# Constant matmuls placed before TensorE's pieces in the first pairs of a linear-attention and MLP kernel

## The chip, the cores and the metric

The kernel runs on one core of a Trainium2 chip. The metric is the device time of one execution in microseconds (us). A core has five engines that work beside one another, each through its own instructions in order: TensorE (PE, matrix products; its weight loads are listed as PEld), VectorE (DVE), ScalarE (ACT), GpSimd (POOL) and SyncE (SP), which here only issues DMAs. Engines wait for one another through semaphores.

## The reference

Inputs q, k, v and f_logit have the shape batch 4, heads 8, sequence 768, head dimension 48. For each batch and head a 48 x 48 state is carried along the sequence:

```python
f = 1.0 / (1.0 + np.exp(-f_logit))
for t in range(S):
    state = f[:, :, t, :, None] * state + np.einsum('bhd,bhe->bhde', k[:, :, t], v[:, :, t])
    y[:, :, t] = np.einsum('bhd,bhde->bhe', q[:, :, t], state)
```

The result is laid out as 3072 tokens of 384 numbers (x) and goes through an MLP with w_in (384 x 2048) and w_out (2048 x 384):

```python
h = x @ w_in
g = 0.5 * (h + np.sqrt(h * h + 4.0))
out = g @ w_out
```

## The kernel before

The 3072 tokens are cut into 24 blocks of 128 tokens, r = 0 to 23, and 12 pairs of blocks, p = 0 to 11. The recurrence is computed by blocks. For each pair:

- SP loads f_logit, q, k and v (`add_load`, L376). In the first three pairs each block has its own pieces (`FINE`).
- ACT makes the logarithms of the gates (exp, then ln: L422, L427), and POOL or DVE splits them into two 16-bit parts, lhi and llo (L430, L433).
- PE forms centred sums of these along the block by a product with a constant triangle, wcent (`m1`, L464 and L465), and the small sums of L470 and L471. ACT takes exponentials of both signs, ea and eap (L478). POOL or DVE multiplies q and k by them (L484) and casts v (L491).

Then follows, for each block, the attention (`add_attention`, `add_state`): transposes of q and k into qkT (L587, `tp`; its copy out of PSUM is L591), scores (L612, `sc`), the mask on DVE (L619, pm), the output y (L633 and L635, `yf`), its cast by ACT or DVE (L642, L644), transposes of y (L677, `yt`) copied by L680, and the state's update (L697 and L700, `kv`, and L704 on DVE, sn). Some pairs' transposes are made by DMA instead (`XBAR`, none of the first five pairs). The MLP takes a pair as 256 tokens: the up-projection in eight halves of four engines' pieces (`half`, L734, six matmuls for each of the eight w_in tiles), the square on ACT (L740, hsq), the root on ACT (L749, r), the sum on DVE (L757, g), and the down-projection in quarters (`quarter`, L777), the copy out (L786, L788) and the store (L792). Exponentials and roots need different ACT tables, which are reloaded between stretches (L831, L833).

POOL also issues the DMAs of the weights, eight tiles of w_in and eight of w_out (L400). They stand in POOL's one order between its other pieces; the first of w_in waits for the v cast of pair 1.

The order of all engines is written out by a planner before anything is emitted (`Plan`, L97 to L274). Every piece of work is an `Op` with an engine, an assumed duration, dependencies, buffers that it takes and uses, and a due time. `Plan.run` walks through time with these assumed durations and picks, engine by engine, the piece that can start first, by due time among those that could start almost at once. The result is the list `P.order`; after that the pieces are emitted in this order:

```python
    P.run()
    for op in P.order:
        ...
            op.emit()
```

Each engine then executes its instructions in this fixed order, and the assumed times play no further part. PSUM has eight banks: five in the ring `hps`, used by the centred sums, the up-projection and the first four blocks' attention (`EARLY`), two in `a` for the later attention, one in `o`.

ident16, a 128 x 128 identity of 16 bits, is made by POOL at the very start and is the constant operand of the transposes.

Of the kernel before, what the change touches and what calls it, by code (L numbers as in the profile page):

```python
# [65 lines left out]

LATE = 11

VDMA = False


class Op:
    __slots__ = ("eng", "dur", "deps", "emit", "due", "allocs", "uses", "end", "kind", "dma", "ins", "done", "kin")

    def __init__(self, eng, dur, emit, deps=(), due=0.0, allocs=(), uses=(), kind=None, dma=None, ins=()):
        self.eng, self.dur, self.emit, self.due, self.kind, self.dma = eng, dur, emit, due, kind, dma
# [20 lines left out]
class Plan:  # L97
# [14 lines left out]
    def __init__(self):  # L112
        self.queues = {}
        self.order = []

    def add(self, queue, eng, dur, emit, p=None, at=None, due=0.0, **kw):
        if isinstance(dur, dict):
            eng = FULL[ENG[queue][p if at is None else at]]
            dur = dur[eng]
        due += SHIFT.get(queue, 0.0) + (0.0 if p is None else BASE[PART[queue]][p])  # L120
        op = Op(eng, dur, emit, due=due, **kw)
        op.kin = queue
        self.queues.setdefault((eng, queue), []).append(op)
        return op

    def ready(self, op):
        t = 0.0
        for d in op.deps:
            if d.end is None:
                return None  # L130
            t = max(t, d.end + (0.0 if d.eng == op.eng and d.dma is None else self.HOP))
        for b in op.allocs:
            r = b.ring
            k = len(r.bufs) - r.n
            if r.ordered and b.seq != len(r.bufs):
                return None

            k += sum(1 for x in op.allocs[:op.allocs.index(b)] if x.ring is r)
            if k >= 0:
                for u in r.bufs[k].users:  # L140
                    if u.end is None:
                        return None
                    t = max(t, u.end + (0.0 if u.eng == op.eng and u.dma is None else self.HOP))
        return t

    def transfer(self, streams, t, until):

# [24 lines left out]
    def run(self):  # L172
# [10 lines left out]
        while left:  # L183
            best = None
            for eng, ks in by_eng.items():
                now = free.get(eng, 0.0)
                cands = []
                for k in ks:
                    if heads[k] < len(self.queues[k]):
                        op = self.queues[k][heads[k]]  # L190
# [59 lines left out]
            if eng == "ACT" and op.kind is not None:  # L250
# [5 lines left out]
                if op.kind[0] == "W":  # L256
                    stretch = op.kind[1]
                    if not any(o.kind == op.kind for o in self.queues[k][heads[k] + 1:]):
                        stretch = None
            free[eng] = op.end = t + dur  # L260
            if eng == "DVE" and op.kin in self.PORT:
                locked = op.end
            if op.dma is not None:
# [14 lines left out]
def kernel(  # L278
# [10 lines left out]
    nc = tc.nc  # L289
# [155 lines left out]
    def add_decays(p, g):  # L445
# [11 lines left out]
        for x, y in pieces(p):  # L457
            n = y - x

            def m1(x=x, y=y):  # L460
                for r in range(x, y):
                    T["ca", p, r] = pp_h.tile([128, 512], FP32, name="hps", tag="hps")
                    ca = T["ca", p, r][:, 0:H * D]
                    nc.tensor.matmul(out=ca, lhsT=wcent, rhs=lhi[p % NL][:, r, :, 0:D], start=True, stop=False)  # L464
                    nc.tensor.matmul(out=ca, lhsT=wcent, rhs=llo[p % NL][:, r, :, 0:D], start=False, stop=True)  # L465
                for r in range(x, y):
                    nl = T["ca", p, r][:, H * D:H * D + 2 * NP].rearrange("p (j s) -> p j s", s=2)
                    for hp in range(NP):
                        o = nl[:, hp, :]
                        nc.tensor.matmul(out=o, lhsT=lhi[p % NL][:, r, 2 * hp:2 * hp + 2, :], rhs=hvec, start=True, stop=False)  # L470
                        nc.tensor.matmul(out=o, lhsT=llo[p % NL][:, r, 2 * hp:2 * hp + 2, :], rhs=hvec, start=False, stop=True)  # L471
# [86 lines left out]
    def add_attention(r):  # L558
# [13 lines left out]
        for xbar in (p in XBAR,):  # L572
            if xbar:
                def tx():
                    nc.sync.dma_start_transpose(out=new("qkT", [128, 2 * NP, C], FP16, 3),
                                                in_=qk[p % NB][:, i].rearrange("p a h d -> p (a h d)"))
                t_ops.append(P.add("xq", "SP", 1.2, tx, deps=[g1, g2], p=p, due=due, allocs=[qkT_b], uses=[qk_b, kk_b], dma=(0.9, 1024)))
            else:
                a_b = bank(r)

                def tp():
                    new("qkT", [128, 2 * NP, C], FP16, 3)
                    tr = psum(r, [128, 2 * NP, C], FP16, "tr")
                    T["tr", r] = tr
                    for s in range(2):
                        for j in range(NP):
                            nc.tensor.transpose(out=tr[:, s * NP + j, :], in_=qk[p % NB][:, i, s, 2 * j:2 * j + 2, :],  # L587
                                                identity=ident16)

                def tc_():  # L590
                    cp[tc_ops[r].eng](out=T["qkT", r], in_=T["tr", r])  # L591

                o = P.add("T", "PE", 0.45, tp, deps=[g1, g2], p=p, due=due, allocs=[a_b, qkT_b], uses=[qk_b, kk_b])
                tc_ops[r] = P.add("T", None, {"DVE": 0.69, "ACT": 1.0}, tc_, at=r, deps=[o], p=p, due=due, uses=[a_b])
                t_ops.append(tc_ops[r])
# [8 lines left out]
        def sc():  # L604
            new("pm", [128, 2, NP, C], FP16, 2)
            for s in range(2):
                T["sc", r, s] = psum(r, [128, NP, C], FP32, "sc")
            qkT = T["qkT", r]
            for j in range(NP):
                for s in range(2):  # L610
                    o = 64 * s
                    nc.tensor.matmul(out=T["sc", r, s][:, j, :], lhsT=qkT[o:o + D, NP + j, :], rhs=qkT[o:o + D, j, :],  # L612
                                     start=True, stop=True)
# [13 lines left out]
        def yf():  # L627
            new("y16", [128, NJ, 128], FP16, 3)
            y = psum(r, [128, NP, 2, D], FP32, "y")
            T["y", r] = y  # L630
            for j in range(NP):
                if c > 0:
                    nc.tensor.matmul(out=y[:, j], lhsT=T["qkT", r][:, j, :], rhs=T["sn", r][:, j], start=True, stop=False)  # L633
                for s in range(2):
                    nc.tensor.matmul(out=y[:, j, s], lhsT=T["pm", r][:, s, j, :], rhs=T["v16", p][:, i, 2 * j + s, :],  # L635
                                     start=(c == 0), stop=(c == 0 or s == 1))
# [26 lines left out]
        for xbar in (p in XBAR,):  # L663
            if xbar:
                def yx():
                    xn()
                    nc.sync.dma_start_transpose(out=xo(), in_=T["y16", r].rearrange("p a b -> p (a b)"))
                op = P.add("xy", "SP", 1.2, yx, deps=[yc_op], p=p, due=due + 6.0, allocs=allocs, uses=[y16_b], dma=(0.4, 384))
            else:
                a_b = bank(r)  # L670

                def yt():
                    xn()
                    t = psum(r, [128, NJ, C], FP16, "yt")
                    T["yt", r] = t
                    for j in range(NJ):
                        nc.tensor.transpose(out=t[:, j, :], in_=T["y16", r][:, j, :], identity=ident16)  # L677

                def ytc():
                    nc.vector.tensor_copy(out=xo(), in_=T["yt", r])  # L680

                o = P.add("YT", "PE", 0.17, yt, deps=[yc_op], p=p, due=due + 6.0, allocs=[a_b] + allocs, uses=[y16_b])
                op = P.add("YT", "DVE", 0.35, ytc, deps=[o], p=p, due=due + 6.0, uses=[a_b])
            xT_ops.setdefault(p, []).append(op)

    def add_state(r, p, due):
# [5 lines left out]
        def kv():  # L692
            T["sn", r + 1] = sp.tile([128, NP, 2, D], FP16, name="sn", tag="sn", bufs=2)
            u = psum(r, [128, NP, 2, D], FP32, "u")
            T["u", r] = u
            if c > 0:
                nc.tensor.matmul(out=u.rearrange("p a b d -> p (a b d)"), lhsT=ident16,  # L697
                                 rhs=T["sn", r].rearrange("p a b d -> p (a b d)"), start=True, stop=False)
# [17 lines left out]
    def add_mlp1(p):  # L716
# [3 lines left out]
        for j4 in range(4):  # L720
            hsq_b, r_b = Buf(ring("hsq", 2)), Buf(ring("r16", 2))
            sq, h_bs = [], [Buf(ring("h", NH)) for _ in range(2)]
            for a in range(2):
                j2 = 2 * j4 + a

                def half(j2=j2, first=a == 0):
                    if first:
                        for x in (j2, j2 + 1):
                            T["h", p, x] = pp_h.tile([128, 512], FP32, name="hps", tag="hps")
                    hb = T["h", p, j2].rearrange("p (a t) -> p a t", a=2)  # L730
                    for a in range(2):
                        jn = 2 * j2 + a
# [31 lines left out]
    def add_mlp2(p):  # L764
        for i in range(PR):
# [3 lines left out]
            for n in range(4):  # L769
                def quarter(n=n, i=i):  # L770
                    if n == 0:
                        if p >= LATE:
                            T["o", p, i] = pp_h.tile([128, DM], FP32, name="o", tag="hps")
                        else:
                            T["o", p, i] = pp_o.tile([128, DM], FP32, name="o", tag="o")
                    for jn in range(4 * n, 4 * n + 4):
                        nc.tensor.matmul(out=T["o", p, i], lhsT=T["g", p][:, jn, i * C:(i + 1) * C],  # L777
                                         rhs=w_out16[jn // 2][:, jn % 2, :], start=(jn == 0), stop=(jn == NN - 1))
# [45 lines left out]
    for op in direct_ops:  # L824
        if AFTER[op.kin[1:]] is not None:
            op.deps.append(dec[AFTER[op.kin[1:]], PR - 1][1])

    P.run()
    for op in P.order:
        if op == "exp":  # L830
            nc.scalar.preload_act_table_set("natural_log_exp_and_others")  # L831
        elif op == "sqrt":
            nc.scalar.preload_act_table_set("sqrt_and_others")  # L833
        else:
            op.emit()


# [28 lines left out]
```

## Time and profile before

| | |
|---|---|
| median of 4 runs | 206.98 us (206.68 to 207.39) |
| the profiled execution | 206.59 us, of which the span from first to last instruction is 204.6 us |
| busy PE / ACT / DVE / POOL | 181.8 / 169.1 / 142.5 / 90.9 us |
| granted TensorE clock | 1.000 |
| DMA | 32.09 MB, mean 157 GB/s |

The profile is one execution. Its page gives the busy time of every engine, the span in 40 slices with the busy share in tenths, the chain of waits that ended last, and the costliest groups of instructions. A line such as "22.69 1.03 PE L587 MATMUL tr<-ident,qk ... x8 [3.45 <-POOL qk L484]" in a timeline means: from 22.69 us on, for 1.03 us, PE ran eight matmuls of line 587 that write tr; it had been idle for 3.45 us before, and what ended the wait was POOL's instruction of line 484. The ends of matmuls are modelled and overlap what follows, so the time that a group of matmuls holds PE is read from its start and the start of the next group. A line of the chain gives start, duration and what was at work: an engine with the tile and the line, a DMA, an engine's queue (SPq, POOLq), or "issue", where nothing that the profile shows was waited for. The granted clock in the profile is one number for a window; it need not show all that makes a matmul slow.

### The profile page before, as it was taken

The numbers are of one execution on the slowest core, as the hardware profiler recorded it, in microseconds if no ns is written. First come the engines' busy times: TensorE is split into PE (matmuls) and PEld (weight loads), VectorE is DVE, ScalarE is ACT, GpSimd is POOL, SyncE is SP. The second block draws the span as 40 slices with busy tenths as digits, with TensorE's granted clock in tenths as the row PEclk, the third lists the DMA queues.
The fourth block names the chain that finished last, engine by engine and source line by source line (L and its number), as shares of the span: only waits on it lengthen the run. The fifth ranks groups of instructions, "written<-read, shape, count | busy, mean of one in ns | idle before, by whom it ended". The sixth has DMA issues, their size and how long they took to land.

```text
span 204.6 us, 4831 instructions
## 1 busy us (share of the span) xinstructions
PE 181.8 (89%) x1870; PEld 133.1 (65%) x1870; DVE 142.5 (70%) x286; ACT 169.1 (83%) x271; POOL 90.9 (44%) x103
## 2 busy tenths in 40 slices
PE   0666488889898998999999999999999999999993
PEld 0344366667676576777777777677777877767761
DVE  5656275697765768998498983989828888944720
ACT  4457217989999999999999999999898899967930
POOL 7171599991049396409960059900089100010010
PEclk9999999999999999999999999999999999999999
DMA  6999999999999999999999897999987812121112
GB/s 125 190 187 188 175 185 183 200 218 196 161 202 188 192 221 185 200 159 230 158 196 227 157 203 156 199 199 190 173 136 162 134 27 62 25 93 41 38 38 77
DMA packets 128102, 32.09 MB, mean 157 GB/s; under 512 B 121088, under 2 KB 127360, under 8 KB 128080
## 3 DMA queue, kind: packets, MB, share of 16 engines
q1 hardware_dynamic: 121744, 25.70, 73.7%
q0 software_dynamic: 6336, 6.10, 15.2%
q8 instruction: 14, 0.23, 0.5%
q14 instruction: 8, 0.07, 0.1%
HBM read 25.17 MB, written 4.72 MB: 146 GB/s over the span
## 4 chain that ended last, share of the span: by engine, by line
PE 63%; POOL 8%; ACT 8%; SPq 7%; DMA 6%; issue 4%; DVE 3%; ACTq 0%; POOLq 0%; DVEq 0%
PE o L777 28%; PE hps L734 23%; SPq L376 7%; DMA w_out<-in_moe_w_out_dram 3%; DMA ld_q<-in_q_dram 3%; PE sc L612 3%; POOL w_in L400 2%; POOL qk L484 2%; ACT r L749 2%; ACT hsq L740 2%; PE y L635 2%; POOL llo L433 2%; PE y L633 1%; PE hps L464 1%; PE hps L465 1%
## 5 line engine op out<-in xcount | busy, mean ns | idle before, releaser
L757 DVE SCALAR_TENSOR_TENSOR g<-hps,r 128x512 f16<-128x512 f32 x96 | 62.2, 685 | 17.1 <-ACT r L749 16.4
L777 PE MATMUL o<-w_out,g 128*128 128x384 f16 x384 | 72.3, 326 | 1.2 <-DVE o_sb L788 0.8
L734 PE MATMUL hps<-xT,w_in 128*128 128x256 f16 x576 | 72.7, 277 | 0.7 <-DMA w_in<-in_moe_w_in_dram 0.7
L734 PEld LDWEIGHTS <-w_in 128*128 128x128 f16 x576 | 55.7, 99 | 11.5 <-DMA w_in<-in_moe_w_in_dram 1.0
L740 ACT ACTIVATE hsq<-hps 128x512 f16<-128x512 f32 x96 | 54.1, 593 | 5.6 <-PE hps L734 4.3
L749 ACT ACTIVATE r<-hsq 128x1024 f16<-128x1024 f16 x48 | 50.8, 1059 | 1.4
L777 PEld LDWEIGHTS <-g 128*128 128x128 f16 x384 | 35.3, 97 | 20.4 <-issue 1.6
L619 DVE TENSOR_TENSOR pm<-sc,mask 128x512 f16<-128x512 f32 x48 | 31.3, 684 | 8.4 <-PE sc L612 8.3
L792 POOL DMA_DIRECT2D out_dram<-o_sb x15 | 8.6, 573 | 59.0 <-DVE o_sb L788 43.2
L484 POOL TENSOR_TENSOR qk<-ld_q,ea 128x768 f16<-128x768 f32 (+1 forms) x10 | 15.8, 1584 | 27.0 <-PE hps L471 14.2
L484 POOL TENSOR_TENSOR qk<-ld_k,eap 128x768 f16<-128x768 f32 (+1 forms) x12 | 18.6, 1546 | 0.9 <-ACT eap L478 0.9
L433 POOL TENSOR_TENSOR llo<-ls,lhi 128x768 f16<-128x768 f32 (+1 forms) x12 | 16.8, 1401 | 2.0 <-PE hps L734 1.5
L491 POOL CAST v<-ld_v 128x768 f16<-128x768 f32 (+1 forms) x13 | 8.7, 677 | 17.2 <-DMA ld_v<-in_v_dram 17.2
L704 DVE TENSOR_TENSOR sn<-u,gam 128x384 f16<-128x384 f32 x20 | 11.0, 551 | 7.3 <-PE u L700 6.6
L422 ACT ACTIVATE ld_f<-ld_f 128x768 f32<-128x768 f32 (+1 forms) x15 | 10.9, 724 | 5.4 <-DMA ld_f<-in_f_logit_dram 5.3
L464 PE MATMUL hps<-lhi,wcent 128*128 128x384 f16 x24 | 8.9, 369 | 6.3 <-POOL lhi L430 5.5
L478 ACT ACTIVATE ea<-hps 128x384 f32<-128x384 f32 x24 | 10.9, 500 | 3.2 <-PE hps L471 3.0
L635 PE MATMUL y<-v,pm 128*128 128x48 f16 x192 | 12.3, 190 | 0.9 <-DVE pm L619 0.9
L587 PE MATMUL tr<-ident,qk 128*128 128x128 f16 x80 | 8.2, 265 | 5.3 <-POOL qk L484 4.4
L635 PEld LDWEIGHTS <-pm 128*128 128x128 f16 x192 | 10.6, 102 | 2.9 <-DVE pm L619 1.1
L612 PE MATMUL sc<-qkT 48*128 48x128 f16 x192 | 10.6, 233 | 1.6 <-DVE qkT L591 0.8
L427 ACT ACTIVATE ls<-ld_f 128x768 f32<-128x768 f32 (+1 forms) x15 | 10.8, 717 | 1.0
(55 smaller groups left out, 209.1 us busy)
## 6 DMA issues: line engine op xcount, KB each, us to landing
ld_f<-in_f_logit_dram SPq DMA_DIRECT2D x24, 192.0 KB, 4.7
ld_k<-in_k_dram SPq DMA_DIRECT2D x24, 192.0 KB, 4.6
ld_q<-in_q_dram SPq DMA_DIRECT2D x24, 192.0 KB, 4.3
ld_v<-in_v_dram SPq DMA_DIRECT2D x24, 192.0 KB, 4.4
out_dram<-o_sb POOLq DMA_DIRECT2D x15, 192.0 KB, 3.8
out_dram<-o_sb SPq DMA_DIRECT2D x9, 192.0 KB, 2.0
w_in<-in_moe_w_in_dram POOLq DMA_DIRECT2D x8, 192.0 KB, 6.7
w_out<-in_moe_w_out_dram POOLq DMA_DIRECT2D x8, 192.0 KB, 7.4
```

The source lines that it names most:

```text
L376: (nc.gpsimd if cast else nc.sync).dma_start(out=T["v16" if cast else name, p][:, r], in_=src_of[name][b][:, c * C:(c + 1) * C, :].rearran ...
L433: eng_of[lg[p, x].eng].tensor_tensor(out=llo[p % NL][:, x:y, :, 0:D], in0=T["ls", p][:, x:y], in1=lhi[p % NL][:, x:y, :, 0:D], op=ALU.subt ...
L484: eng_of[mu[p, x, i].eng].tensor_tensor(out=qk[p % NB][:, x:y, i, :, 0:D], in0=T[name, p][:, x:y], in1=T[e, p][:, x:y], op=ALU.mult)
L612: nc.tensor.matmul(out=T["sc", r, s][:, j, :], lhsT=qkT[o:o + D, NP + j, :], rhs=qkT[o:o + D, j, :], start=True, stop=True)
L619: nc.vector.tensor_tensor(out=T["pm", r][:, s], in0=T["sc", r, s], in1=mask16.unsqueeze(1).broadcast_to([128, NP, C]), op=ALU.mult)
L635: nc.tensor.matmul(out=y[:, j, s], lhsT=T["pm", r][:, s, j, :], rhs=T["v16", p][:, i, 2 * j + s, :], start=(c == 0), stop=(c == 0 or s == 1))
L704: nc.vector.tensor_tensor(out=T["sn", r + 1], in0=T["u", r], in1=gam[b % 2][:, c].unsqueeze(3).broadcast_to([128, NP, 2, D]), op=ALU.mult)
L734: nc.tensor.matmul(out=hb[:, a, :], lhsT=w_in16[j2][:, j, a * 128:(a + 1) * 128], rhs=T["xT", p][:, j, :], start=(j == 0), stop=(j == NJ - 1))
L740: nc.scalar.activation(out=T["hsq", p, j4][:, a], in_=T["h", p, j2], func=AF.Square, scale=1.0)
L749: nc.scalar.activation(out=T["r16", p, j4], in_=T["hsq", p, j4], func=AF.Sqrt, scale=0.25, bias=1.0)
L757: nc.vector.scalar_tensor_tensor(out=T["g", p][:, jn:jn + 2, :].rearrange("p a t -> p (a t)"), in0=T["h", p, 2 * j4 + a], scalar=0.5, in1= ...
L777: nc.tensor.matmul(out=T["o", p, i], lhsT=T["g", p][:, jn, i * C:(i + 1) * C], rhs=w_out16[jn // 2][:, jn % 2, :], start=(jn == 0), stop=( ...
```

## The change

The planner stores the planned start of each piece. A new method, `warm`, then walks through PE's pieces in their order and gives each a number, `heat`, by the idle time that the plan shows ahead of it: the first piece gets 0.8 of its gap at 0.08 us each, later ones 0.7 of a gap over 0.3 us at 0.058 us each, as long as they start before 45 us in the plan. When a PE piece is emitted, as many products of the identity with itself are put before it, into the PSUM tile that the piece is about to write. The real matmul starts its accumulation anew, so the products leave nothing behind. Before the transposes (`tp`, `yt`) they are transposes of the identity, elsewhere 128 x 128 matmuls of 128 columns. The orders of all engines stay as they were.

```diff
+WARM = 45.0
...
+    def warm(self):
+
+
+        end = 1.6
+        for op in self.order:
+            if not isinstance(op, str) and op.eng == "PE":
+                gap = op.start - end
+                if end < 2.0:
+                    op.heat = int(0.8 * gap / 0.08)
+                elif gap > 0.3 and op.start < WARM:
+                    op.heat = int(0.7 * gap / 0.058)
+                end = op.start + op.dur
...
             free[eng] = op.end = t + dur
+            op.start = t
...
                     ca = T["ca", p, r][:, 0:H * D]
+                    if r == x:
+                        heat(ca[:, 0:C])
                     nc.tensor.matmul(out=ca, lhsT=wcent, rhs=lhi[p % NL][:, r, :, 0:D], start=True, stop=False)
...
                     T["tr", r] = tr
+                    for _ in range(P.heat):
+                        nc.tensor.transpose(out=tr[:, 0, :], in_=ident16, identity=ident16)
...
                 T["sc", r, s] = psum(r, [128, NP, C], FP32, "sc")
+            heat(T["sc", r, 0][:, 0, :])
...
             T["y", r] = y
+            heat(y.rearrange("p a b d -> p (a b d)")[:, 0:C])
...
                     T["yt", r] = t
+                    for _ in range(P.heat):
+                        nc.tensor.transpose(out=t[:, 0, :], in_=ident16, identity=ident16)
...
             T["u", r] = u
+            heat(u.rearrange("p a b d -> p (a b d)")[:, 0:C])
...
                             T["h", p, x] = pp_h.tile([128, 512], FP32, name="hps", tag="hps")
+                    heat(T["h", p, j2][:, 0:C])
...
+                        heat(T["o", p, i][:, 0:C])
...
+    def heat(t):
+        for _ in range(P.heat):
+            nc.tensor.matmul(out=t, lhsT=ident16, rhs=ident16, start=True, stop=True)
+
     P.run()
+    P.warm()
...
+            P.heat = op.heat
             op.emit()
```

In the emitted program this makes 246 products, 492 rows with their weight loads, before 20 of PE's pieces. In PE's order they stand as follows:

| before | products |
|---|---|
| centred sums of block 0, block 1 | 49, 8 |
| transposes, scores of block 0 | 14 (transposes), 13 |
| transposes of block 1, y of block 0 | 6 (transposes), 9 |
| y, transposes of y of block 1 | 10, 12 (transposes) |
| transposes, scores of block 2 | 17 (transposes), 13 |
| state's update by block 2, y of block 2 | 5, 5 |
| y, transposes of y of block 3 | 17, 11 (transposes) |
| centred sums of block 5 | 12 |
| up-projection of pair 0: second, third tile | 6, 6 |
| y of block 4 | 13 |
| up-projection of pair 0: fifth tile | 17 |
| up-projection of pair 1: first tile | 3 |

More of the change, by code (lines that the diff above doesn't have):

```diff
@@ L67 @@
 LATE = 11
+WARM = 45.0
 VDMA = False
 class Op:
-    __slots__ = ("eng", "dur", "deps", "emit", "due", "allocs", "uses", "end", "kind", "dma", "ins", "done", "kin")
+    __slots__ = ("eng", "dur", "deps", "emit", "due", "allocs", "uses", "end", "kind", "dma", "ins", "done", "kin", "heat", "start")
     def __init__(self, eng, dur, emit, deps=(), due=0.0, allocs=(), uses=(), kind=None, dma=None, ins=()):
@@ L114, in __init__ @@
         self.order = []
+        self.heat = 0
     def add(self, queue, eng, dur, emit, p=None, at=None, due=0.0, **kw):
@@ L122, in add @@
         op.kin = queue
+        op.heat = 0
         self.queues.setdefault((eng, queue), []).append(op)
```

## The prediction

> **What bounds the kernel now.** I read the page first (shares and the 40 slices), then the chain of waits in order of time for the first 70 us, then the timelines of TensorE (PE), ScalarE (ACT) and GpSimd (POOL) there, and last what SyncE's (SP) queue waits for.
>
> ```profile
> PE 181.8 (89%) x1870; PEld 133.1 (65%) x1870; DVE 142.5 (70%) x286; ACT 169.1 (83%) x271; POOL 90.9 (44%) x103
> ...
> PE   0666488889898998999999999999999999999993
> ```
>
> A slice is 5.1 us. PE is idle at the start and nearly full from the tenth slice on: the change works only where PE has room, in the first 45 us. Who sets the time there is told by the chain:
>
> ```profile
> 15.96 5.55 DMA ld_q<-in_q_dram
> ...
> 21.64 0.79 POOL qk L484
> ...
> 37.64 0.71 POOL w_in L400
> 38.38 1.66 POOL llo L433
> 40.03 0.67 POOL w_out L400
> 40.70 6.88 DMA w_out<-in_moe_w_out_dram
> ...
> 47.62 0.48 PE o L777 x2
> 48.10 1.32 PE hps L734 x12
> 49.45 0.61 ACT hsq L740
> 50.08 1.06 ACT r L749
> ```
>
> The chain has no PE in its first 47 us. It runs through SP's loads to a landing at 21.5, through POOL's work and weight issues to 40.7, through a weight's landing to 47.6, then through ACT to 69 and PE to the end. PE in that time:
>
> ```profile
> 22.69 1.03 PE L587 MATMUL tr<-ident,qk 128*128 128x128 f16 x8 [3.45 <-POOL qk L484]
> 23.52 0.53 PE L697 MATMUL u<-sn,ident 128*128 128x384 f16 x1
> ...
> 33.03 2.72 PE L734 MATMUL hps<-xT,w_in 128*128 128x256 f16 x12
> 35.54 1.06 PE L587 MATMUL tr<-ident,qk 128*128 128x128 f16 x8
> ...
> 42.35 0.61 PE L587 MATMUL tr<-ident,qk 128*128 128x128 f16 x8
> 42.80 0.82 PE L734 MATMUL hps<-xT,w_in 128*128 128x256 f16 x6
> 44.30 0.83 PE L734 MATMUL hps<-xT,w_in 128*128 128x256 f16 x6 [0.69 <-DMA w_in<-in_moe_w_in_dram]
> ```
>
> Take starts, not durations. Eight transposes take 0.83 us at 22.69 (104 ns each) but 0.45 at 42.35 (56 ns); twelve up-projection matmuls take 2.51 us at 33.03 (209 ns each) but 1.31 later (109 ns). So PE runs at about half speed until some 37 us and at full speed after, though the granted clock reads 1.000 in every window. And in the last row PE waits for a weight.
>
> ```profile
> 31.30 0.48 ACT L642 CAST y<-y 128x384 f16<-128x384 f32 x1 [3.85 <-PE y L635]
> ...
> 33.21 0.49 ACT L478 ACTIVATE ea<-hps 128x384 f32<-128x384 f32 x1 [0.65 <-PE hps L471]
> ...
> 45.17 0.60 ACT L740 ACTIVATE hsq<-hps 128x512 f16<-128x512 f32 x1 [0.49 <-PE hps L734]
> ```
>
> These are ACT's only waits between 31 and 57 us; it is dense otherwise (22.8 of 24 us busy from 33 to 57). The last one is the weight of 44.30 passed on.
>
> **The change part by part.** It removes and reorders nothing. On PE it puts 246 constant products (186 matmuls, 60 transposes) ahead of 20 of the planned pieces. By the transposes' rows one costs 56 ns on a fast PE and 104 ns on a slow one: 13.8 or 25.6 us in all. DMAs, queues and the other engines' instructions are the same. What is queued behind a product is the real piece that it stands before, so lateness is what counts.
>
> *To 22.7 us: 138 products (49, 8, 14, 13, 6, 9, 10, 12, 17).* The first need only the identity, ready at 1.30. PE's idle pieces before 22.69 are 5.55 + 0.91 + 0.79 + 0.93 + 0.51 + 0.65 + 3.45 = 12.8 us, 11.5 after 1.30. Fast, 138 x 56 ns = 7.7 us fit. All slow, 14.4 us leave 2.9 us of lateness at the transposes of 22.69. I take no lateness: 49 products in a row are 5.1 us even when slow, longer than the 4 us of dense work from 33.03 after which PE was seen fast. What hides any small lateness is the landing of ld_q at 21.5, for which POOL sat idle 5.33 us; SP's queue ahead of it waits only for earlier DMAs. Nothing can be gained before that landing either.
>
> *22.7 to 33 us: 63 products (13, 5, 5, 17, 11, 12).* Fast they cost 3.5 us. PE is busy 8.34 of these 10.3 us at half speed; at full speed some 4 us go, and waits of 0.46 + 0.93 + 0.57 us take products too. So the y piece before ACT's 31.30 comes perhaps 1 us earlier. What is late next is POOL: the centring matmul of the next block needs llo, which POOL ends at 32.34, and it already started at 32.45. So ACT's ea at 33.21 gains about 0.3 us. POOL itself waits for none of this: its qk at 33.09 starts when its weight issue ends, 0.5 us after ACT's eap is done. All slow, 63 x 104 = 6.6 us less the 2.0 us of waits make the 33.21 row 4.6 us later.
>
> *33 to 45 us: 42 products (6, 6, 13, 17) and 3 more.* At 56 ns the 42 cost 2.35 us. Speed gives back 12 x 100 ns at 33.03, 8 x 48 ns at 35.54, and of the 1.42 us of the next six matmuls all but 6 x 109 ns: 1.2 + 0.4 + 0.8 = 2.4 us. They cancel, and a wait of 0.75 us at 40.08 holds the 13. PE reaches the last up-projection weight no later than before and stands there until it lands. Its issue is POOL's at 37.57, behind POOL work without a gap from 25.5 us on. So the 0.49 us wait of ACT stays or grows by the 0.3 us gained above, and 45.17 is unmoved. The 3 last products (0.17 us) precede matmuls that end at 46.0 for a square at 46.76: hidden; without that cover 0.17 us.
>
> *From 45 us on* PE's instructions are the same. The second down-projection weight still lands at 47.6, ACT is full to 69, PE after it.
>
> *The unseen price: DVE meeting POOL.* Where DVE's pieces move up, they collide elsewhere with POOL. At 32.78 such a DVE product took 2.41 us instead of 0.55, and POOL's own at 34.86 took 1.18 instead of 1.00. So POOL, which sets the weights, can gain 0.2 us or lose 0.2 to 0.4. I take zero, between near ends.
>
> *A rule against it.* The Trainium skill's page "TensorE: Matmul & The Clock Gate", Part 4, says that transposes do not count as work that holds the array's clock up; the 17 before the row of 22.69 are transposes. No row here separates this. By the rule PE would be slow again from 22.69 for one or two windows, which Part 1 gives as 3.4 us each; as an estimate from that page the sum is 207.0 if one is enough and some 208 with two. The sum below goes by the rows alone, 207.0.
>
> Sum: the profiled execution took 206.59 us, span 204.6 and 2.0 around it; change 0.0 (ends -0.2 and +0.4). The median of the runs is 206.98, 0.39 above it: **207.0 us**. One measurement of this kernel tells about 0.3%, 0.62 us, from no change.
>
> **The rivals.**
>
> *A weight that lands sooner lets ACT go (faster).* Landings of w_in spread from 4.5 to 7.6 us; with 4.5 us the last would be there at 42.1 and no wait remain. Then ACT keeps the 0.3 us, gains the 0.49 and 0.15 us (the squares of 48.83 take 1.22 us where other pairs take 1.07): 0.9 us, 206.1. For it: the wait is only 0.69 us and is read from one execution. Against: POOL's issue times do not move, SP's loads fill the DMA engines as before, and ACT's fullness caps the gain.
>
> *The products run slow, or the plan's gaps are not there (slower).* One mechanism: PE does not speed up or falls back, so each product costs 104 ns. Place: the 63 between 22.7 and 33 us. ACT's row of 33.21 comes 4.6 us later; 0.49 us are absorbed at 45.17, 4.1 us reach the end: 211.1. It decides once that row is over about 0.5 us late, which is also POOL's slack at 33.09. If PE is slow only to 28 us, I get that row 0.5 us late, and nothing is left at the end. For it: the present kernel is dense from 24.83 to 29.4 and still slow afterwards. Against: those are short matmuls (48 and 96 columns), the products are 128 wide. Here too belongs that the change doesn't do what it says: PE stays slow.
>
> *Code or port (slower).* The instruction queue carries 0.23 MB in 14 packets; PE gets 492 more rows in the stretch where the DMA engines are full. One fetch that PE had to wait out would cost like a load, whose landing takes 4.3 to 4.7 us, less the slack: up to 4 us; with a POOL collision more or less, 1 us, 208.0. For it: DMA digits of 9. Against: no row of PE waits for code now, and 24 rows in 1.3 us are fetched in time later.
>
> **How the numbers follow.** Hidden: 0.50 (206.5 to 207.5, from -0.2 to +0.4 and the spread of the runs). Weight sooner: 0.20. Slow products: 0.18. Code or port: 0.12. Faster 0.20, same 0.50, slower 0.30. The low end is the weight case's 206.1 with the spread of the runs, 205.8; the high end takes half of the slow products' way, 209.1; about 1 in 10 is left above and less below.
>
> **What would show it.** Right: PE's transposes at 22.7 at 56 ns each, the matmuls at 33 at 109 ns, PE's wait for w_in near 44 longer than 0.69 us, ACT's square still near 45.2, w_out still landing near 47.6. The clock step is wrong if transposes at 22.7 take 104 ns; the hiding step is wrong if POOL's issue at 37.57 or ACT's square at 45.17 has moved by more than 0.5 us. The prediction fails if POOL's chain between 25 and 40 us hangs on PE more than its rows say, or if PE pauses inside a run of products.

## The result and the profile after

The changed kernel takes 208.09 us in the median (206.90 to 210.58, 32 runs), the kernel before 206.99 us (51 runs): slower by a ratio of 1.0054, with a 95% interval of 1.004 to 1.0067. The time lies in the stated range, but not in the part of it that was called likeliest ("hidden", within 0.3%). It lies where the rival "code or port" put it, at 208.0. The longest of the 32 runs, 210.58 us, was in a slower state of the core; such runs (one more in each of runs 4 and 6 below, two in run 10) stand in the medians and spreads given here, but not in the ratios.

The profiled execution took 207.69 us, with a span of 205.7 us, 1.1 us over that of before. Its page, with the busy times, the slices of PE, the clock that was granted, and the queue that brings instructions:

```profile
PE 191.2 (93%) x2116; PEld 145.3 (71%) x2116; DVE 143.1 (70%) x286; ACT 168.8 (82%) x271; POOL 90.7 (44%) x103
...
PE   7858986989898998999999999999999999999993
...
PEclk9995899999999999999999999999999999999999
...
q8 instruction: 16, 0.26, 0.6%
```

PE is busy from the first slice. The granted clock now shows a dip in the fourth and fifth slice (15 to 25 us). The last line had 14 packets before: the 492 new rows are two more packets of 16 KB. They belong to PE, since nothing else was added.

The chain of waits of the changed kernel, in order of time:

```profile
9.88 2.08 SPq L394
...
16.53 4.64 DMA ld_q<-in_q_dram
...
21.30 0.94 POOL qk L504
...
24.28 1.73 issue
26.03 0.50 POOL v L511
...
37.90 6.83 DMA w_in<-in_moe_w_in_dram
...
44.78 0.84 PE hps L762 x6
45.65 0.60 ACT hsq L768
```

It takes the same way as before, loads, POOL, a weight, ACT, and every station from the v cast on is later: the cast at 26.03 instead of 25.48, the last w_in issue at 37.90 instead of 37.57, the matmuls that wait for it at 44.78 instead of 44.30, the square at 45.65 instead of 45.17. PE had done what was hoped of it. Its timeline after, and ACT's:

```profile
22.88 0.61 PE L609 MATMUL tr<-ident,qk 128*128 128x128 f16 x8
23.33 0.33 PE L724 MATMUL u<-sn,ident 128*128 128x384 f16 x1
...
33.29 0.81 PE L762 MATMUL hps<-xT,w_in 128*128 128x256 f16 x6
33.94 0.50 PE L859 MATMUL hps<-ident 128*128 128x128 f16 x6
...
44.78 0.83 PE L762 MATMUL hps<-xT,w_in 128*128 128x256 f16 x6 [0.77 <-DMA w_in<-in_moe_w_in_dram]
```

```profile
30.26 0.48 ACT L666 CAST y<-y 128x384 f16<-128x384 f32 x1 [3.66 <-PE y L659]
...
33.46 0.49 ACT L498 ACTIVATE ea<-hps 128x384 f32<-128x384 f32 x1 [1.95 <-PE hps L491]
```

The transposes at 22.88 take 56 ns each, the matmuls at 33.29 108 ns: full speed. The y cast comes 1.0 us earlier than before. But ea comes 0.25 us later, because it waits for POOL's llo, and POOL is behind.

Where POOL lost its time is seen in the windows of 5 us. The first line is the kernel before, the second the kernel after, both from 10 to 15 us (columns: window, its length, busy time of PE, PEld, DVE, ACT and POOL with instructions, granted clock, DMA share, GB/s):

```profile
10.00:15.00 5.00, 3.00 (x36) 2.07 (x36) 2.86 (x5) 2.66 (x7) 3.52 (x6) 1.00 1.42 187
```

```profile
10.00:15.00 5.00, 3.23 (x62) 2.53 (x58) 2.61 (x5) 1.68 (x4) 2.49 (x5) 1.00 0.99 159
```

In a stretch that holds only loads, the DMA rate falls from 187 to 159 GB/s. An instruction packet lies in that window after and not before, and SP's issue at 9.88 takes 2.08 us where its neighbours take about 1. This first packet alone does not make the v cast late. The kernel before has a packet too, between 15 and 20 us, also with a long issue beside it, and ld_q lands no later after the change than before (21.17 against 21.51 us). What the kernel before does not have is a second packet before the v cast. It comes between 20 and 25 us. SP's queue, first the long issue of the kernel before, then that beside the second packet after:

```profile
18.16 2.13 SPq L376 DMA_DIRECT2D ld_q<-in_q_dram  x1
```

```profile
21.81 2.00 SPq L394 DMA_DIRECT2D ld_v<-in_v_dram  x1
```

The last of the four issues of ld_v then starts at 24.82 us instead of 24.03. Counted over the first 25 us, the instruction queue reads, before and after:

```profile
q8 instruction: 1, 0.02, 0.3%
```

```profile
q8 instruction: 2, 0.03, 0.7%
```

Of the 1.1 us, the ACT table load near 57 us (57.35 before, 57.73 after) carries 0.4; the rest came between 100 and 154 us in this execution, and no run shows why.

### The profile page after: what moved, and what is told of

Its sections match the earlier page's. It is cut to its first block, busy times and chain, and to the rows that moved or that the text cites. A ratio compares the mean times of both kernels' runs of the same rounds, so it can differ in the third digit from the quotient of the medians.

```text
span 205.7 us, 5322 instructions
## 1 busy us (share of the span) xinstructions
PE 191.2 (93%) x2116; PEld 145.3 (71%) x2116; DVE 143.1 (70%) x286; ACT 168.8 (82%) x271; POOL 90.7 (44%) x103
## 3 DMA queue, kind: packets, MB, share of 16 engines
q1 hardware_dynamic: 121744, 25.70, 73.4%
## 4 chain that ended last, share of the span: by engine, by line
PE 55%; ACT 9%; DMA 9%; SPq 7%; POOL 7%; DVE 6%; issue 4%; ACTq 0%; POOLq 0%; DVEq 0%
PE o L806 24%; PE hps L762 22%; SPq L394 7%; DMA w_in<-in_moe_w_in_dram 3%; ACT r L777 3%; ACT hsq L768 3%; POOL w_in L418 3%; POOL qk L504 2%; DMA xT<-y 2%; PE sc L635 2%; DVE g L785 2%; DMA ld_q<-in_q_dram 2%; DVE pm L642 2%; PE y L659 1%; PE y L657 1%
## 5 line engine op out<-in xcount | busy, mean ns | idle before, releaser
L762 PE MATMUL hps<-xT,w_in 128*128 128x256 f16 x576 | 70.9, 273 | 1.7 <-DMA w_in<-in_moe_w_in_dram 1.4
L762 PEld LDWEIGHTS <-w_in 128*128 128x128 f16 x576 | 54.6, 98 | 12.3 <-DMA w_in<-in_moe_w_in_dram 1.8
L859 PEld LDWEIGHTS <-ident 128*128 128x128 f16 x186 | 13.2, 111 | 1.5 <-POOL ident masks.py:199 1.4
L668 DVE CAST y<-y 128x384 f16<-128x384 f32 x16 | 8.8, 553 | 4.1 <-PE y L659 4.0
L659 PE MATMUL y<-v,pm 128*128 128x48 f16 x192 | 11.6, 185 | 0.0
L498 ACT ACTIVATE eap<-hps 128x384 f32<-128x384 f32 x24 | 11.0, 514 | 0.0
L659 PEld LDWEIGHTS <-pm 128*128 128x128 f16 x192 | 9.9, 98 | 1.0 <-DVE pm L642 0.2
```

What stands on the lines that cost most here:

```text
L498: nc.scalar.activation(out=T[name, p][:, r].rearrange("p h d -> p (h d)"), in_=T["ca", p, r][:, 0:H * D], func=AF.Exp, scale=sign)
L762: nc.tensor.matmul(out=hb[:, a, :], lhsT=w_in16[j2][:, j, a * 128:(a + 1) * 128], rhs=T["xT", p][:, j, :], start=(j == 0), stop=(j == NJ - 1))
L859: nc.tensor.matmul(out=t, lhsT=ident16, rhs=ident16, start=True, stop=True)
```

## Experiments

Two theories were set against each other first. *Code*: the extra rows need instruction packets, which travel on the DMA engines that the loads already fill; loads and weights land later, and POOL and ACT follow. *Clock*: in other executions than the profiled one PE falls back to half speed at a bad place, so that the products make it late. Every ratio is against runs of the kernel before on the same chip in the same job; the times of different jobs are not compared. A ratio, given with its 95% interval, need not be the quotient of the two medians. The runs are numbered 1 to 12; "run 4" is the changed kernel again.

**1. The code without the work.**

```diff
     def heat(t):
         for _ in range(P.heat):
-            nc.tensor.matmul(out=t, lhsT=ident16, rhs=ident16, start=True, stop=True)
+            nc.tensor.matmul(out=t[:, 0:2], lhsT=ident16, rhs=ident16[:, 0:2], start=True, stop=True)
```

The products before transposes are written in the same way into the 32-bit view of their tile.

> The same 246 products, with as many instructions, but each streams 2 columns instead of 128 (the ones before transposes become 2-column matmuls too). They cost PE next to nothing and cannot speed it up. Code theory (the 492 extra rows need two more 16 KB instruction packets in the first 45 us, 4 instead of 2, each holding one DMA engine for 1.4 to 1.7 us while the loads need all sixteen): about +1.1 us, 208.1. Clock theory (PE falls back to half speed for 3.4 us windows at unlucky places and the products then make PE late): no change, 207.0, and a spread like the kernel before.

Measured: 207.18 us beside 206.64, ratio 1.0021 (1.0006 to 1.0035), spread 206.72 to 207.79. The code with little work costs something, 0.4 us by the ratio, where 1.1 us was expected. It is not code alone: 246 products at some 27 ns take 6.6 us of PE's idle time, and the chain of waits runs mostly through PE from 35.71 to 43.87 us. The chain has an issue by SP of 1.57 us at 10.14, not much longer than one of 1.47 us at 2.58 without a packet near it; the v cast starts at 25.70.

**2. Twice the code.** As 1, with `range(2 * P.heat)`.

> 492 products of 2 columns: twice the code, still almost no PE time. Code theory: about four more instruction packets than before in the first 45 us, +2 us, 209. Clock theory: no change, 207.0.

Measured (7 runs): 208.14 us beside 206.64, ratio 1.0063 (1.0041 to 1.0086). The direction is the code theory's, and the clock theory is excluded for this kernel: PE is at half speed to 37 us, as before. Three packets fall into the first 25 us. The chain of waits:

```profile
5.74 1.96 SPq L394
...
13.44 2.07 SPq L394
```

There are now two long issues, 7.7 us apart. The v cast follows at 26.22. One reservation: 492 products at some 27 ns also cost PE up to 13 us of its idle time, so this run is not code alone.

**3. The work with a third of the code.**

```diff
     def heat(t):
-        for _ in range(P.heat):
-            nc.tensor.matmul(out=t, lhsT=ident16, rhs=ident16, start=True, stop=True)
+        k = t.shape[1] // 128
+        for _ in range(P.heat // k):
+            nc.tensor.matmul(out=t[:, 0:128 * k], lhsT=ident16, rhs=ident16.unsqueeze(1).broadcast_to([128, k, 128]),
+                             start=True, stop=True)
```

Each place hands over the whole tile that is about to be written. Of the 77 products, 37 then have 512 columns, 17 have 384, and the 23 before transposes of y only 128: together nine tenths of the columns of the changed kernel.

> The same number of product columns in 77 instead of 246 products (384 or 512 columns each, as wide as the tile that is about to be written): PE's time and its clock as in the changed kernel, but 154 extra rows instead of 492, 10 KB instead of 31 KB. Code theory: +0.2 to +0.4 us, 207.3. Clock theory: the same as the changed kernel, about 208.1, with its wide spread.

Measured: 206.54 us in the median beside 206.64; ratio 1.0016 (0.999 to 1.0041). Seven runs lie at 206.12 to 206.56, five at 207.18 to 208.30. The median is the code theory's, and lower still; the upper group is neither theory's. The profiled execution belongs to the upper group, and it shows what was late there. SP's queue and POOL's v cast of the fourth pair:

```profile
35.31 17.73 SPq L394 DMA_DIRECT2D ld_f<-in_f_logit_dram  x4
53.08 4.31 SPq L394 DMA_DIRECT2D ld_v<-in_v_dram  x2
```

```profile
61.73 0.82 POOL L511 CAST v<-ld_v 128x768 f16<-128x768 f32 x1 [15.28 <-DMA ld_v<-in_v_dram]
```

Before, the four ld_f issues took 10.94 us and the cast came at 58.17; in the profile of the changed kernel they took 13.81 us, and the cast came at 59.33. So loads that compete with the weights were late, at a granted clock of 1.00 throughout the start: not the clock.

**4. The changed kernel again.**

> The changed kernel once more, beside the three variants on the same chip, and a second profiled execution. Both theories: about 208.1 us. Code theory: an instruction packet again near 11, 22 and 31 us with a load that lands late beside it. Clock theory: the time goes with the share of half speed, and ACT's exponentials near 33 us or the last w_in square near 45 us are late because of PE, not because of a DMA.

Measured: 207.98 us beside 206.64, ratio 1.0066 (1.0038 to 1.0094), 207.04 to 210.49. The second profiled execution has the long issues again (2.18 us at 9.78, 2.32 us at 20.63), the v cast at 25.89, the last w_in issue at 38.10 and the square at 46.32, behind a wait of PE for w_in of 1.31 us. The clock theory's sign, ACT late because of PE and not of a DMA, is not there. One reservation: the profile puts the wait of the v cast at 25.89 down to DVE (pm), and only that of the next one, at 27.54, to the load of v. In the same job as run 3, with nearly the same work on PE, three times the rows make the ratio 1.0066 instead of 1.0016; the two intervals hardly overlap (1.0038 to 1.0041).

**5 and 6. Full products early, or late.** Same 246 instructions as in 1; the two runs differ in which products are 128 columns wide. `P.piece` counts the pieces of PE that have products ahead of them.

```diff
+            n = 128 if P.piece <= 9 else 2     # 5: early;  6: P.piece > 9
+            nc.tensor.matmul(out=t[:, 0:n], lhsT=ident16, rhs=ident16[:, 0:n], start=True, stop=True)
```

> The 246 products in the same places and with the same code; the 138 before the first nine pieces (to 22.7 us) stream 128 columns, the 108 after them 2 columns. (All are matmuls, none transposes.) Theory A, code alone costs, and full products after 22.7 us cost because they run where weights and loads compete: like the 2-column version, about +0.5 us on the kernel before, spread 0.4. Theory B, the start's products and the clock that they set cost: like the changed kernel, +1.1 to +1.4 us, spread 0.9.

> The opposite: the 138 early products stream 2 columns, the 108 after 22.7 us stream 128. Theory A: like the changed kernel, +1.1 to +1.4 us with the wide spread. Theory B: about +0.5 us.

Measured in one job beside 207.29 us: early 208.31 us, ratio 1.0046 (1.0016 to 1.0077); late 207.81 us, ratio 1.0023 (0.9996 to 1.005), both with a wide spread (206.85 to 209.92 and 207.16 to 211.57). Theory A, that the late products are what costs beyond the code, is not borne out: it wanted +1.1 to +1.4 us for the late version, whose interval ends at +1.0 us, and the early ones did not come out cheaper. Both medians are nearly as theory B has them, but it is not shown either, since the intervals overlap. Both have two packets in the first 25 us, and v casts at 26.05 and 26.62.

**7. Wide products, early only.** As 3, with products before the first nine pieces alone: 43 products, 86 rows.

```diff
-            P.heat = op.heat
+            P.piece += 1 if op.heat else 0
+            P.heat = op.heat if P.piece <= 9 else 0
```

> Only the products before the first nine pieces, as 43 wide ones (86 extra rows, a third of a packet), nothing after 22.7 us. Theory A: no cost, -0.3 to +0.1 us on the kernel before. Theory B: +0.5 to +0.9 us.

Measured beside 207.29 us: 207.01 us, ratio 0.9972 (0.9951 to 0.9992), 206.53 to 207.53. In the same job as 5, with nearly the same early work on PE, but 86 rows instead of 492: the early products as such cost nothing, against theory B. PE fell back to half speed in it (granted clock 0.50 from 25 to 35 us), and it is no slower for that. One packet before 25 us, v cast at 25.50.

**8. Code alone, where PE has nothing to do.** As 1, but 150 products before the first piece and none after (`P.heat = 150 if op.heat and P.piece == 1 else 0`).

> 150 products of 2 columns, all before the first piece, where PE is idle from 1.4 to 5.5 us (150 at 27 ns are 4.1 us), and none later: 300 rows, 1.2 instruction packets, and no other work of PE moves. Code theory: packets come earlier and one more falls into the first 45 us, +0.2 to +0.3 us. If products cost only by PE's time between the pieces: 0.0.

Measured: 207.92 us beside 207.29, ratio 1.0022 (0.9996 to 1.0048). By the ratio this is +0.5 us, more than the expected +0.2 to +0.3, but the interval holds these and just includes no change. The trace is clearer than the time. One line of the chain of waits, and one of POOL's timeline:

```profile
5.70 2.25 SPq L394
```

```profile
26.43 0.50 POOL L511 CAST v<-ld_v 128x384 f16<-128x384 f32 x1 [1.38 <-DMA ld_v<-in_v_dram]
```

The long issue has moved to 5.70, ahead of any other change in PE's work, and the rate from 5 to 10 us is 163 GB/s (190 before). The v cast is 0.95 us late.

**9. Run 7 again.**

> The 43 wide products before the first nine pieces once more. Code theory (no packet more before the v cast near 25.5 us, so nothing is late): -0.6 to 0.0 us on the kernel before. If the earlier gain was an accident of one chip: +0.3 us or more.

Measured: 206.89 us beside 207.54, ratio 0.9985 (0.996 to 1.001). Not slower; whether faster is not settled by this run.

**10. Run 3 again.**

> All 77 wide products once more, because its first runs fell into two groups, near -0.3 and near +1.3 us. If full products after 22.7 us disturb the loads in some executions: two groups again, median between -0.3 and +0.8 us. If the second group was an accident: one group at -0.3 us.

Measured: 207.76 us beside 207.54, ratio 1.0005 (0.9972 to 1.0038), 206.42 to 209.60, without a clear gap between groups. The wide spread is there again, and the median is in the expected bounds. In the profiled execution everything at the start was early: v cast at 25.18, last w_in issue at 37.08, PE's matmuls behind it at 43.96.

**11. Only the twelve wide products before the first piece.** As 7 with `P.piece <= 1`; 24 rows.

> Only the 12 wide products before the very first piece (24 extra rows). If an early fast clock gains by itself: the start is fast for some 7 us and may fall back; -0.3 to 0.0 us. If no packet and no later product means no effect: 0.0 us.

Measured: 208.27 us beside 207.54, ratio 1.0034 (1.0 to 1.0067). Neither expectation: PE did fall back (granted clock 0.50 from 10 to 35 us), there is no packet more, the v cast is at 25.40, the table load at 57.51, and yet the median is 0.7 us higher; in the profiled execution the time is lost after 154 us. This run is not explained.

**12. The code of run 7 without its work.** As 7, each product 2 columns wide.

> The 43 products before the first nine pieces with 2 columns each: the code of the wide early version without its PE time and without a faster PE. If the early wide version's gain comes from a faster PE: 0.0 us here. If it comes from the 86 rows moving the instruction packets: the same -0.3 to -0.6 us.

Measured: 206.67 us beside 207.54, ratio 0.9963 (0.9941 to 0.9985), 206.19 to 207.44. This is faster than the kernel before in this job, where that one spread from 206.63 to 209.23 us, and PE is at half speed for most of the time to 35 us in it, since nothing keeps it busy. So a gain like that of run 7 does not need a faster PE; whether there is one was not tested again. In its trace the v cast stands at 25.36 and the wait for w_in is as long as before:

```profile
44.24 0.83 PE L760 MATMUL hps<-xT,w_in 128*128 128x256 f16 x6 [0.76 <-DMA w_in<-in_moe_w_in_dram]
```

The second instruction packet falls into 30 to 35 us here and into 35 to 40 us in the kernel before. That the shift of the packets makes the gain fits, but was only seen beside it.

The profiled executions side by side:

| kernel | extra rows | packets to 25 us | v cast at | table load near 57 us | span | ratio |
|---|---|---|---|---|---|---|
| before | 0 | 1 | 25.48 | 57.35 | 204.6 |  |
| 11 | 24 | 1 | 25.40 | 57.51 | 206.2 | 1.0034 |
| 7, 9 | 86 | 1, 1 | 25.50, 25.83 | 57.60, 57.81 | 204.9, 205.3 | 0.9972, 0.9985 |
| 12 | 86 | 1 | 25.36 | 57.14 | 204.4 | 0.9963 |
| 3, 10 | 154 | 1, 1 | 25.41, 25.18 | 58.29, 56.88 | 206.3, 204.8 | 1.0016, 1.0005 |
| 8 | 300 | 2 | 26.43 | 58.45 | 206.5 | 1.0022 |
| after, 4 | 492 | 2, 2 | 26.03, 25.89 | 57.73, 58.33 | 205.7, 205.7 | 1.0054, 1.0066 |
| 1 | 492 | 2 | 25.70 | 57.95 | 205.2 | 1.0021 |
| 5, 6 | 492 | 2, 2 | 26.05, 26.62 | 58.16, 58.62 | 206.0, 207.8 | 1.0046, 1.0023 |
| 2 | 984 | 3 | 26.22 | 58.52 | 206.1 | 1.0063 |

With two or three packets in the first 25 us, all seven casts are at 25.70 or later, and all six kernels have a ratio above 1, four of them with an interval above 1. With one packet, six of seven casts are at 25.50 or earlier, and no ratio has an interval above 1 (that of run 11 begins at 1.0). The span goes with the cast: without runs 3, 10 and 11 it never falls as the v cast gets later, from 204.4 us at 25.36 to 207.8 at 26.62. It is one execution of each kernel; 3 and 11 are long in spite of an early cast, so the late v cast is not the only loss.

## Why the prediction was right, and where it was wrong

The range, 205.8 to 209.1 us, held the measured 208.09, but not for the reason behind the forecast of 207.0, products that stay hidden. The time came out at the price of the rival that was given 0.12, whose mechanism the profiles do not show, and below a high end that was taken from slow products, which they do not show either. That the range held is luck in good part.

- **PE at half speed to 37 us, and fast with the products: right.** 56 ns and 108 ns at 22.9 and 33.3 us were forecast as 56 and 109. The 49 first products took from 1.36 to 5.99 us, 94 ns each, between the two prices. PE did fall back once, near 15 to 22 us (granted clock 0.55 from 15 to 21).
- **Hidden before 22.7 us by ld_q: right.** POOL's first product of pair 1 starts at 21.30, not later than before, and the transposes at 22.88, 0.2 us late. PE itself was 0.5 us late there: from the start of POOL's product to the transposes it took 1.05 us before and 1.58 us after. POOL's next wait, at the v cast, is for a load and not for them.
- **22.7 to 33 us: right for PE, wrong for POOL.** The y cast was forecast 1 us earlier, and came 1.0 us earlier. The forecast gain of 0.3 us at ea became a loss of 0.25, because llo was late.
- **Products and speed cancel from 33 to 45 us: right.** PE stood and waited for the last w_in tile, 0.77 us instead of 0.69.
- **"DMAs, queues and the other engines' instructions are the same": this is the step that failed.** The instruction queue had two more packets, and what it was to leave alone, POOL's issues and the landing of w_in, moved by 0.3 to 0.5 us in the first profile and by 0.5 to 1.2 us in the second (run 4). The sign that was named for it, more than 0.5 us at POOL's issue or ACT's square, was just missed in the first (0.33 and 0.48) and met in the second (0.53 and 1.15). Run 8 shows the later loads with code alone, run 1 puts 0.21% on the code with its little work, run 2 with twice the code 0.63%, and run 3 with a third of it none that is clear.
- **The rival "code or port": right in place and price (208.0), wrong in how.** It let PE wait for a late fetch. No row of PE names a wait for code in these traces; the loads pay: SP's issue beside an early packet takes 1.6 to 2.7 us in the chains of runs 1, 2, 4, 6, 8 and of the changed kernel instead of about 1, and behind a second such packet the load stream does not catch up before the v cast that POOL needs.
- **The rival "slow products": not what the profiles show**, where PE was fast from 22.9 us on (run 4: granted clock 0.92 from 20 to 25 us and 1.00 after). It is not excluded as a share of the spread: without the run of 210.58 us, the eight runs with a mean clock of 0.982 or less average 208.6 us, the other 23 average 208.0. But at one clock, 0.992, the times reach from 206.90 to 208.86, so most of the spread is something else.
- **The rival "a weight lands sooner": not in the changed kernel.** Run 10's execution is what it would look like (43.96, square at 44.83), with fewer rows.
- **DVE meeting POOL**, priced at -0.2 to +0.4 us: POOL's product that took 1.18 us took 1.01, a gain of 0.17; this end was met.
- **The rule on transposes** of the Trainium skill's page "TensorE: Matmul & The Clock Gate", Part 4, that they do not count as work that keeps the clock up: the clock of run 5, where all products are matmuls, has the same course as the changed kernel's to 25 us (0.52 against 0.56 from 15 to 20, 0.80 against 0.76 from 20 to 25). No harm by the transposes is seen; PE was fast at 22.88 right behind 17 of them. No run tests transposes alone.

What stays open: the code with little work (run 1) costs 0.21%, the changed kernel 0.54% to 0.66%. Wide products with little code (3, 10) show no clear cost but widen the spread, as the changed kernel's runs do; the late load in run 3's execution is one such case. Why products and code together cost more than each, the longer times of run 11, and what is lost after 100 us were not settled.

## What to carry to other kernels

Instructions are traffic. In a stretch where the DMA engines are full and an engine's loads are on the chain, every 250 rows or so bring a 16 KB packet (984 rows brought four). With one more of them ahead of it, or two, a load that POOL needed came 0.2 to 1.1 us later here than in the kernel before, where kernels with one packet lie 0.65 us apart among themselves. To keep an engine busy there, use few wide instructions (77 instead of 246) rather than many small ones; that took the clear loss away here, but brought no gain. And before making an engine faster, ask which wait would end last then: PE was at full speed as planned, and the weights that it waited for came no sooner.

## What the runs showed of the hardware that was not expected

- Instruction packets of 16 KB each travel in the program's DMA time: 14 in the kernel before, 16 with 492 more rows, 18 with 984. The rows of the instruction queue show them coming during the run.
- One such packet goes with a fall of the load rate from 187 to 159 GB/s over 5 us, although it is only 0.016 of some 0.9 MB; in the same window it is 164, 151 and 154 GB/s in runs 4, 5 and 6, and 184 to 188 in runs 3, 7 and 9 to 12, which have no packet from 5 to 15 us.
- The granted clock reads 1.00 in the kernel before through 37 us in which PE ran at half speed; it shows the half only after PE had once been fast.
- 86 rows of matmuls with two columns each made the kernel 0.4% faster in one job on one chip (0.9941 to 0.9985), with PE slow to 35 us for the most part.
